# Running the first kernel block's preparation beside the last pass of the stage before it

## The chip, the cores and the metric

The kernel runs on one core of one Trainium2 chip. Times are device microseconds (us) of that core, from the first to the last instruction. "Before" and "changed" are the two kernels. Every number comes from timed runs or from the profile of one execution; a profiled execution lasts about as long as an unprofiled one. TensorE's *granted clock* is given as a share of full speed.

## The reference, cut to what matters

```python
def forward(x, w_r, w_i, A_re, A_im, B_re, B_im, C_re, C_im, log_dt, Dskip, gate_w):
    g = sigmoid((x * gate_w).sum(-1, keepdims=True))
    # 2D stage: a spectral filter over sequence (2048) and channels (1024)
    a = irfft2(rfft2(x) * (w_r + 1j * w_i))
    # kernel loop: K[d,l] = Re sum_n C dB exp(dt A l), then a long convolution
    K = einsum("dn,dnl,dn->dl", Cc, exp(dt * A * l), dt * Bc).real
    b = irfft(rfft(x, 4096) * rfft(K, 4096))[:2048] + x * Dskip
    return g * a + (1 - g) * b
# the kernel returns this function's gradients for grad_out
```

The kernel first does the 2D stage, forward and backward. Then a loop over eight blocks of 128 channels builds `K`. The change is at the seam of the two.

## The kernel before

The 2D stage ends with its backward half. `middle(True)` multiplies the spectra and writes one gradient, `gw`, to memory. `last_bwd` is the last pass, 16 steps. In each step TensorE runs 8 matmuls for step h+1 and 4 for step h; VectorE and ScalarE evict one half each of the first product, and ScalarE evicts the second product.

```python
def last_d(bwd, h):
    ...  # 8 matmuls of V and DP into pd
    Ue = wps["Ue"].tile([P, 2, 512], dt.bfloat16, name="Ue", bufs=2)
    nc.vector.tensor_copy(out=Ue[:, 0, :], in_=pd[:, 0, :])
    nc.scalar.activation(out=Ue[:, 1, :], in_=pd[:, 1, :], func=ACT.Copy)
    return Ue

def last_n(bwd, h, Ue):
    ...  # 4 matmuls of B1, nB1 and Ue into pa
    och = wps["och"].tile([P, D], dt.bfloat16, name="och", bufs=2)
    nc.scalar.activation(out=och[:], in_=pa[:].rearrange("p a b -> p (a b)"), func=ACT.Copy, ...)
    nc.sync.dma_start(out=scr.rearrange("(r h) d -> r h d", h=H16)[:, h, :], in_=och[:])

def last_bwd():
    Ue = last_d(True, 0)
    for h in range(H16):
        nxt = last_d(True, h + 1) if h + 1 < H16 else None
        last_n(True, h, Ue)
        Ue = nxt
...
    open_pools(s2_, ("a_mid2", ("Xf", "gw", "Z", ...)), ("a_last", ("Ue", "och")))
    middle(True)
    last_bwd()
```

The memory of all that is handed to the kernel loop when the stage ends. Only then does the loop prepare block 0: `OP` (decays times sines, 9 operations on VectorE and 6 sines on ScalarE), `EA` (32 exponentials on ScalarE), the weights `wb` (on GpSimd, from a table that a transfer brings into `bc`), `wO` (`OP` times `wb`, 5 operations on VectorE), and `AN` in four units.

```python
def weights(bi, OP):
    bc = kw.tile([P, 4, P], dt.bfloat16, name="bc", bufs=1)
    nc.gpsimd.dma_start(out=bc[:], in_=nlb_scr[2:6, :, dsl]...)
    dtk = kw.tile([P, P], dt.float32, name="dtk", bufs=1)
    nc.gpsimd.dma_start(out=dtk[:], in_=dt_scr[:, dsl])
    TTp(out=bc[:, 0:2, :], in0=bc[:, 0:2, :], in1=dtk..., op=ALU.mult)
    ...  # seven more small operations on GpSimd give wb and wv
    wO = kw.tile([P, 2, NA, P], dt.bfloat16, name="wO")
    nc.vector.tensor_tensor(out=wO[:], in0=OP[:], in1=wb[:, 0:2, :]..., op=ALU.mult)
    ...  # two more products and sums on VectorE
    return wO
...
AN = new_an()
OP = sin_o(0, EO)
EA = exps_a(0)
wO = weights(0, OP)
for q in range(4):
    sin_a(0, q, AN, EA)
for bi in range(DC):        # block bi runs on TensorE while block bi+1 is prepared
    ...
```

## Time and profile before

| | before |
|---|---|
| median of 3 runs | 1442.45 us (1437.49 to 1445.57) |
| profiled span | 1437.5 us |
| backward middle stage, first product to its last copy | 295.9 to 396.7 |
| last backward pass, to the start of its last eviction | 396.7 to 441.9 |
| block 0's first transpose on TensorE | 478.4 |
| block 0 done on TensorE: its first `KT` on VectorE | 516.5 |

No engine bounds the whole. The first part of the page of the kernel before gives busy time, share of the span and number of instructions by engine:

```profile
PE 1070.7 (74%) x7161; PEld 736.9 (51%) x7187; DVE 1143.5 (80%) x1897; ACT 841.8 (59%) x1279; POOL 239.2 (17%) x489
```

So one reads the seam by stretches. This is the busy time by stretch, kernel before; the first row names the columns.

```profile
core 0: us, PE busy (x) PEld busy (x) DVE busy (x) ACT busy (x) POOL busy (x), PEclk, DMA share, GB/s
287.00:400.00 113.00, 93.97 (x573) 52.72 (x580) 78.28 (x180) 43.77 (x49) 23.38 (x50) 1.00 0.63 115
400.00:443.00 43.00, 40.08 (x183) 23.37 (x184) 12.93 (x21) 24.39 (x33) 21.11 (x36) 1.00 0.39 132
443.00:478.00 35.00, 0.00 (x0) 0.00 (x0) 29.36 (x25) 29.63 (x50) 11.32 (x11) 0.50 0.55 216
478.00:520.00 42.00, 21.33 (x142) 17.22 (x142) 36.27 (x37) 32.84 (x58) 9.71 (x11) 0.54 0.37 129
```

In the pass (second stretch) TensorE is busy 40 of 43 us and VectorE only 13. In the third stretch TensorE does nothing at all, while VectorE and ScalarE prepare block 0. In the fourth, block 0 runs at about half the clock.

The timeline of the kernel before shows single instructions: start, duration, engine and line, output and input, and in brackets the idle time before it and what ended that.

```profile
394.33 0.82 POOL L857 DMA_DIRECT2D bc<-nlb_scr  x1
...
404.79 0.69 DVE L495 CAST Ue<-p 128x512 bf16<-128x512 f32 x1 [1.97 <-PE p L492]
...
405.52 0.60 ACT L496 ACTIVATE Ue<-p 128x512 bf16<-128x512 f32 x1 [1.15 <-DVE Ue L495]
406.01 1.02 ACT L506 ACTIVATE och<-p2i 128x1024 bf16<-128x1024 f32 x1
406.55 0.56 POOL L870 TENSOR_SCALAR wv<-wv 128x128 f32<-128x128 f32 x1
...
442.90 1.28 ACT L123 ACT_TABLE_LOAD   x1
444.20 1.04 ACT L123 ACTIVATE OP<-ti__4270,pi_b 128x896 bf16<-128x896 uint16 x1
...
478.41 0.33 PE L888 MATMUL trp<-ident,AN 128*128 128x128 bf16 x1 [36.64 <-DVE AN L818]
```

The last row is the prize: TensorE waits 36.6 us for `AN`. The first row: GpSimd asks for block 0's table at 394, so `wb` is ready at about 406, long before anybody wants it.

In the middle stage VectorE waits for the following; the view of the waits of the kernel before, 295.87 to 396.69, gives for each line and releaser the us in total, the number and the longest:

```profile
DVE UV L638 <- ACT UV L640: 18.9, 6, 3.2
DVE m L594 <- ACT Gs L586: 8.5, 6, 5.2
DVE gw L607 <- DMA out_dram<-gw: 1.8, 1, 1.8
DVE m L594 <- DMA out_dram<-gw: 0.6, 2, 0.3
```

### The profile page before, as it was taken

What the parts mean: (1) busy time and instruction counts of PE and PEld (TensorE: products, weight loads), DVE (VectorE), ACT (ScalarE), POOL (GpSimd) and SP (SyncE); (2) the same over time, 40 slices, a digit from 0 to 9 for tenths busy, and PEclk for the clock granted to TensorE, in tenths of its full rate; (3) what the DMA queues carried; (4) which work ended last, traced back from release to release, by engine and by line L of the source; (5) the groups of instructions that cost most, each with busy time, mean ns of one, the idle gap of its engine ahead of it and who ended that gap; (6) DMA issues with size and microseconds to landing.
All of it is one profiled execution on the core that took longest, in us unless ns stands there. A gap on an engine that the chain in (4) does not pass through costs nothing. (4 is left out here: it accounts for less than half of the span.)

```text
span 1437.5 us, 20147 instructions
## 1 busy us (share of the span) xinstructions
PE 1070.7 (74%) x7161; PEld 736.9 (51%) x7187; DVE 1143.5 (80%) x1897; ACT 841.8 (59%) x1279; POOL 239.2 (17%) x489
## 2 busy tenths in 40 slices
PE   3968887688892356856964979688898887688973
PEld 1434444344451244645752756466666654566752
DVE  5668999667726979788878887388999999789997
ACT  2563455534358687686687554356666564677750
POOL 5101110012251312101100010301203032122110
PEclk9879999899996556855965958899999998699996
DMA  4445574247646242434432547888979664887751
GB/s 146 154 131 158 167 214 169 110 119 122 104 121 255 81 150 88 156 147 147 180 132 95 193 157 242 286 124 161 215 132 282 72 209 73 257 318 262 244 165 30
DMA packets 153067, 236.06 MB, mean 164 GB/s; under 512 B 26371, under 2 KB 100739, under 8 KB 149766
## 3 DMA queue, kind: packets, MB, share of 16 engines
q1 hardware_dynamic: 133766, 184.95, 45.4%
q0 software_dynamic: 12960, 48.25, 10.9%
q10 hardware_dynamic: 6240, 1.57, 0.5%
q8 instruction: 56, 0.92, 0.3%
q14 instruction: 45, 0.37, 0.2%
HBM read 126.80 MB, written 107.66 MB: 163 GB/s over the span
## 5 line engine op out<-in xcount | busy, mean ns | idle before, releaser
L889 PE MATMUL pK<-wO,AN 128*128 128x84 bf16 x512 | 101.0, 343 | 23.2 <-DVE st L997 21.0
L1066 ACT ACTIVATE Vt<-f 128x1024 bf16<-128x1024 f32 (+1 forms) x72 | 64.5, 930 | 91.5 <-PE f L1155 52.9
L888 PE MATMUL trp<-ident,AN 128*128 128x128 bf16 x512 | 76.3, 277 | 47.3 <-DVE AN L818 41.5
L1434 DVE TENSOR_TENSOR pd<-Tsb,ORJ 128x5376 bf16<-128x5376 bf16 x32 | 94.0, 2949 | 8.2 <-PE pr L1440 7.0
L924 PE MATMUL kx<-Kc,TK 128*128 128x256 bf16 x680 | 96.0, 284 | 2.7 <-DVE spk L932 1.5
L1321 ACT ACTIVATE Tsb<-pT 128x704 bf16<-128x704 f32 x112 | 76.7, 754 | 26.2 <-PE pT L1315 26.0
L889 PEld LDWEIGHTS <-AN 128*128 128x128 bf16 x512 | 75.7, 151 | 29.5 <-issue 24.2
L888 PEld LDWEIGHTS <-AN 128*128 128x128 bf16 x512 | 61.3, 159 | 55.7 <-DVE AN L818 42.9
L1164 PE MATMUL pq<-TKT,PY 128*128 128x321 bf16 x544 | 85.7, 304 | 0.8 <-DVE PY L1134 0.6
L549 PE MATMUL p<-TD,UV 128*128 128x512 bf16 x240 | 66.0, 400 | 24.0 <-DVE Y L553 16.0
L1440 PE MATMUL pr<-pd,ident 128*128 128x256 bf16 x504 | 70.6, 292 | 16.4 <-DVE pd L1434 16.3
L1066 ACT ACTIVATE XG<-f 128x1024 bf16<-128x1024 f32 (+1 forms) x72 | 68.2, 983 | 23.0 <-PE f L1104 9.3
L1191 PE MATMUL f<-Vr,S1i 128*128 128x256 bf16 x256 | 69.1, 389 | 6.6 <-DVE Vr L1072 6.6
L924 PEld LDWEIGHTS <-TK 128*128 128x128 bf16 x680 | 62.8, 101 | 20.9 <-issue 4.3
L629 PE MATMUL p2i<-T,Z 128*128 128x512 bf16 x224 | 60.4, 390 | 9.8 <-DVE Z L596 4.4
L1315 PEld LDWEIGHTS <-A2t 128*128 128x128 bf16 x512 | 47.3, 105 | 38.3 <-issue 25.7
L1164 PEld LDWEIGHTS <-PY 128*128 128x128 bf16 x544 | 53.4, 99 | 25.8 <-DVE PY L1134 1.6
L1440 PEld LDWEIGHTS <-ident 128*128 128x128 bf16 x504 | 51.3, 105 | 27.9 <-DVE pd L1434 14.7
L997 DVE CAST st<-pK 128x1024 bf16<-128x1024 f32 x40 | 48.6, 1218 | 19.7 <-PE pK L992 19.5
L1121 DVE TENSOR_TENSOR m<-XG,kb 128x1024 bf16<-128x1024 bf16 (+1 forms) x80 | 46.8, 606 | 20.8 <-ACT XG L1066 16.2
L1315 PE MATMUL pT<-BD,A2t 128*128 128x176 bf16 x448 | 52.0, 251 | 12.8 <-ACT Tsb L1321 7.5
L492 PE MATMUL p<-DP,UV 128*128 128x512 bf16 x250 | 61.1, 385 | 0.6 <-DVE UV L638 0.3
(833 smaller groups left out, 3161.5 us busy)
## 6 DMA issues: line engine op xcount, KB each, us to landing
at<-A SPq DMA_DIRECT2D x32, 512.0 KB, 2.6
st<-st SPq DMA_DIRECT2D x64, 256.0 KB, 2.9
A2t<-at SPq DMA_DIRECT2D x32, 512.0 KB, 7.5
Sg<-st SPq DMA_DIRECT2D x24, 512.0 KB, 7.9
on_scr<-OP SPq DMA_DIRECT2D x8, 1344.0 KB, 8.2
ORJ<-on_scr POOLq DMA_DIRECT2D x8, 1344.0 KB, 9.2
spk<-spk SPq DMA_DIRECT2D x64, 128.0 KB, 1.8
kb<-spk SPq DMA_DIRECT2D x32, 256.0 KB, 5.4
```

Of the source, the lines that this page charges most:

```text
L492: nc.tensor.matmul(pd[:, eo, :], lhsT=V[:, eo * 2 + c_, b_, :, :].rearrange("p k n -> p (k n)")[:, h::H16], rhs=DP[:, eo * 2 + c_, b_, :], ...
L549: nc.tensor.matmul(ps[:, eo, :], lhsT=U[:, dc, (eo * K16 + k1r) * P:(eo * K16 + k1r + 1) * P], rhs=TD[:, dc, eo, :], start=(dc == 0), stop ...
L888: nc.tensor.transpose(trp[:, comp, cc, :], AN[:, comp, :, c], ident[:, :])
L889: nc.tensor.matmul(pK[:, c4, cc * 4 * NA:(cc + 1) * 4 * NA], lhsT=AN[:, comp, :, c], rhs=wO[:, comp, :, c::32].rearrange("p a q -> p q a") ...
L924: nc.tensor.matmul(px[:, comp, :], lhsT=TK[ci][:, k1, comp, :], rhs=Kc[:, ci, :], start=(ci == 0), stop=(ci == 4 and comp == 1))
L1066: nc.scalar.activation(out=out, in_=in_, func=ACT.Copy)
L1164: nc.tensor.matmul(pq[:, half, 0:NLG // 2], lhsT=PY[:, k_, comp, 256:384], rhs=TKT[:, p0 + k_, comp, half * (NLG // 2):(half + 1) * (NLG / ...
L1191: nc.tensor.matmul(py[:, hh, :, :], lhsT=S1i[:, f_, :], rhs=Vr[:, :, 2 * (hq * HQ + hh) + f_, :], start=False, stop=(f_ == 1), skip_group_ ...
L1315: nc.tensor.matmul(pT[:, cc, 0:4 * NX], lhsT=A2[:, comp, cl * N:(cl + 1) * N], rhs=BD[:, c0_ + cc, :, :].rearrange("p q x -> p (q x)"), st ...
L1321: nc.scalar.activation(out=to_, in_=ti_, func=ACT.Copy)
L1434: TT(out=pd[:], in0=Tsb[:, k_].rearrange("p (g a) d -> p g a d", g=2)[:, :, 0:NA, :], in1=O_.unsqueeze(1).to_broadcast([P, 2, NA, P]), op= ...
L1440: nc.tensor.matmul(pr[:], lhsT=idt[:], rhs=pd[:, :, a_, :], start=(k_ == 0 and a_ == 0), stop=(k_ == 1 and a_ == NA - 1))
```

## The change

The tiles of the last pass move to memory that outlives the 2D stage (a pool `late`, into which the loop's `TK` tables are loaded after the pass). So the loop's memory is free before the pass. `EA` and `OP` of block 0 are written into the program behind the middle stage. `last_bwd` becomes a generator, and `wO` and `AN` are woven between its steps. Cut to its core:

```diff
+        late = lctx.enter_context(tc.tile_pool(name="late", bufs=1, ...))
-            DP = ac.tile([P, 4, 2, 512], dt.bfloat16, name="DP")
+            DP = late.tile([P, 4, 2, 512], dt.bfloat16, name="DP")
+            XS = late.tile([P, 4, 2048], dt.int32, name="UV2")      # tables' integers; later UV2, later TK
+            UO = late.tile([P, 4, D], dt.bfloat16, name="UO")
...
-                Ue = wps["Ue"].tile([P, 2, 512], dt.bfloat16, name="Ue", bufs=2)
+                Ue = UO[:, h % 2, :].rearrange("p (a b) -> p a b", a=2)
...
-                och = wps["och"].tile([P, D], dt.bfloat16, name="och", bufs=2)
+                och = UO[:, 2 + h % 2, :]
...
                     last_n(True, h, Ue)
                     Ue = nxt
+                    yield h
...
-                tp = s1_.enter_context(tc.tile_pool(name="a_tmp", bufs=1, ...))
+                # the first tables take their integers from XS; kci, kcf, n2k too
...
+            bctx.close()
+            kps[0] = ectx.enter_context(tc.tile_pool(name="k_prep", bufs=1, side="right", ...))
             with ExitStack() as s2_:
                 middle(True)
-                last_bwd()
+                EA = new_ea()
+                exps_a(0, EA)
+                OP = sin_o(0, EO0)
...
-            OP = sin_o(0, EO)
-            EA = exps_a(0)
+            lb = last_bwd()
+            next(lb)
+            next(lb)
             wO = weights(0, OP)
             for q in range(4):
+                next(lb)
+                next(lb)
                 sin_a(0, q, AN, EA)
+            for _ in lb:
+                pass
+            psctx.close()
+            load_tk()
```

Besides, the skip row is loaded by blocks. Hardly any work is added or removed.

## The prediction

> **What bounds the kernel now.** No engine bounds the whole span: the page's first part has VectorE at 80%, TensorE at 74%, ScalarE at 59%. The change concerns the seam at 400 to 480 us (timeline and busy-time-by-stretch views):
>
> - 400 to 443, the last backward pass: 16 steps of 2.59 us, set by TensorE (busy 40.1 of 43). VectorE is busy 12.9 (a 0.69 us eviction a step, "idle 1.90 <-PE"), ScalarE 24.4.
> - 443 to 478, preparation of kernel block 0: TensorE does nothing. Its first transpose waits 36.6 us for the last product into AN, one of the two longest waits of 400 to 480. VectorE is busy 29.4 of 35, ScalarE 29.6, mostly in series: OP's sines, 32 exponentials (9.9 us), AN's sines.
>
> Afterwards a block takes 42 us, with VectorE busy 36 to 37: close to its limit.
>
> **What the change does.** Almost no work is removed or added; it is moved. The pass's tiles get memory that outlives the 2D stage, so the loop's memory is free before the pass.
>
> - On ScalarE EA's exponentials (9.9 us), OP's six sines (6.2) and two table loads (1.28 each), and on VectorE OP's nine operations (3 x (1.09 + 0.62 + 1.08) = 8.4) can run from about 290 us, when the turn's buffers are free. They fall into the backward middle stage (287 to 400), where ScalarE is idle 69 us and VectorE 35, with a 3.15 us VectorE gap in nearly every 13 us round.
> - wO (2.95 + 4 x 1.55 = 9.2 us) and AN's four units (about 3.1 us VectorE and 2.3 ScalarE each) go beside the pass. They need 22 us of VectorE, which has 30 idle there, and 9 of ScalarE, which has 19. GpSimd has wb by 406 already today.
> - Added: eight small loads of the skip row. The TK loads stay behind the pass; the first spectrum reads TK at 562, so they are free.
>
> **What lies on the critical path.** The TensorE gap from 441.4 to 478.4, 37 us, less:
> - 5 to 6 us by which fillers stretch the pass. Towards VectorE, TensorE has some 1.7 us of slack per step (12 matmuls 2.59, minus 0.69 and signalling): 1.2 us pieces cost little, wO's 2.95 us piece about 1. ScalarE has 1.62 of 2.59 us taken per step; a 1.15 us sine makes it 2.77, some tenths of a us for each of 8 to 14 sines.
> - 1 to 2 us in the middle stage, about 1 us to hand PSUM over.
>
> The first transpose should come at about 448. Some of block 1's OP may also be done beside the pass, worth 2 to 3 us. I expect 31 us in all, and nothing gives it back: the later stages are as busy as before.
>
> Predicted: 1411 us, range 1398 to 1425. Faster by over 2% (below 1413.6): 0.57; within 2%: 0.41; slower by over 2%: 0.02. It stands close to the threshold.
>
> **What would show each step right or wrong.** In the timeline: Exp and OP's sines on ScalarE before 400, the middle stage's rounds still 13.0 us; the pass's steps at 2.6 to 3 us with AN's and wO's work on VectorE between evictions; first AN transpose at 445 to 452, its wait under 5 us; blocks still about 42 us; from the first spectrum on, everything earlier by the same 30 us.
>
> **What would make it wrong.** The new tiles may reuse memory that is released late, so that sines wait after all. Fillers may be put before critical evictions, so that middle or pass grows by 10 us. Blocks 0 and 1 may wait for something else (block 1's sines, a DMA), so that the earlier start ends in a longer block. The reverse: block 1 fully prepared beside the pass, worth up to 8 us more.

## The result, and the profile after

The changed kernel took 1425.67 us (median of 4 runs, 1420.54 to 1426.91); the kernel before 1441.98 in the same rounds (1437.49 to 1445.57). The ratio is 0.9882, with a 95% interval of 0.9845 to 0.9919. A ratio is the mean time of one kernel's fast runs over that of the other's of the same rounds, so it is not quite the ratio of the medians quoted. The gain is 16 us, about half of the 31 predicted: faster, but within 2%. All outputs are right.

The profile answers to the marks shown above. I read them from the timeline, in two traces of the unedited changed kernel (the second comes from the experiment `changed_again`):

| us | before | changed | changed, again | gain (mean) | predicted |
|---|---|---|---|---|---|
| start of the backward middle | 295.9 | 304.2 | 302.9 | -7.7 | 0 |
| backward middle | 100.8 | 108.4 | 106.5 | -6.6 | -1 to -2 |
| last pass, to the start of its last eviction | 45.2 | 60.4 | 60.0 | -15.0 | -5 to -6 |
| pass to block 0's first transpose | 36.6 | -0.3 | -0.3 | +36.9 | +37, less 1 for PSUM |
| block 0, first transpose to `KT` | 38.1 | 28.5 | 28.7 | +9.5 | +2 to +3 |
| sum: first `KT` at | 516.5 | 501.2 | 497.7 | +17.0 | 31 |

The gap on TensorE is gone entirely, and block 0 got faster than I thought. From the end of the middle stage to the first `KT` the kernel gained 31.3 us (119.8 before, 88.6 and 88.3 changed): the predicted number, by another sum. But 7 us were lost within the middle, and 8 before it.

The 8 us can be placed. The 2D stage has a middle in its forward half too, from its first product `m` to its last copy on ScalarE. Its first product comes no later in the changed kernel (105.00 and 104.32 us in the two traces) than before (105.99), and from its end to the start of the backward middle the time is the same (93.3 before, 93.7 and 93.3 changed). The forward middle itself took 96.6 us before and 105.6 and 105.2 changed. Its busy time by stretch, before and changed, with the columns of above:

```profile
105.99:202.57 96.58, 81.18 (x495) 46.24 (x501) 85.61 (x141) 41.21 (x45) 13.26 (x41) 0.96 0.59 166
```

```profile
105.00:210.56 105.56, 87.00 (x529) 48.55 (x528) 94.16 (x151) 43.62 (x48) 12.48 (x43) 0.97 0.58 164
```

VectorE, the third engine, is the busiest in both, and has 8.6 us more to do there in the changed kernel: six more operations on the tables' angles (`ti`), two more `to` and two more copies of `Y`, which lay outside this stretch in the kernel before, fall into it. That fits the 9 us that the stage grew by; no experiment moved this work out again, so the place of the early loss is shown and its cause is only argued.

The busy time by stretch, changed kernel, in the stretches shown of before:

```profile
287.00:400.00 113.00, 88.87 (x496) 48.61 (x495) 83.87 (x181) 57.51 (x85) 18.19 (x41) 0.95 0.58 129
400.00:443.00 43.00, 33.45 (x187) 18.31 (x186) 29.49 (x43) 19.55 (x24) 22.19 (x28) 0.92 0.40 89
443.00:478.00 35.00, 30.03 (x149) 18.56 (x148) 33.82 (x33) 28.67 (x36) 23.57 (x27) 0.95 0.54 197
478.00:520.00 42.00, 30.12 (x210) 25.22 (x209) 28.53 (x33) 34.55 (x65) 7.36 (x8) 0.63 0.62 222
```

TensorE now works in the third stretch. But in the first two its clock fell to 0.95 and 0.92: it stood still somewhere there, and the next view shows where. In the third stretch VectorE is busy 33.8 of 35 us, so it may now bound the end of the pass; the run wb_ready below tests that.

The timeline of the changed kernel around the pass, with start, duration and waits as before:

```profile
414.96 0.82 POOL L871 DMA_DIRECT2D bc<-nlb_scr  x1 [4.96 <-PE p2i L663]
...
421.69 0.68 POOL L874 TENSOR_TENSOR bc<-bc,dtk 128x256 bf16<-128x256 bf16 x1 [5.36 <-DMA dtk<-dt_scr]
...
425.58 0.41 POOL L882 CAST wb<-wv 128x256 bf16<-128x256 f32 x1
...
426.02 2.96 DVE L887 TENSOR_TENSOR wO<-OP,wb 128x5376 bf16<-128x5376 bf16 x1 [5.50 <-POOL wb L882]
...
426.78 2.59 POOL L884 TENSOR_SCALAR wv<-wv 128x128 f32<-128x128 f32 x1
...
429.64 0.61 PE L534 MATMUL p2i<-UO,B 128*128 128x512 bf16 x1 [5.42 <-DVE UO L528]
...
431.32 3.57 PE L525 MATMUL p<-DP,UV 128*128 128x512 bf16 x8
...
438.18 1.89 PE L525 MATMUL p<-DP,UV 128*128 128x512 bf16 x8
...
472.69 0.31 PE L902 MATMUL trp<-ident,AN 128*128 128x128 bf16 x1
```

Read it from the top. The table for `bc` is asked for at 414.96, not at 394, because GpSimd waits there for a matmul of the middle stage (`PE p2i`). So `wb` is ready at 426.0. VectorE stands 5.5 us before `wO`, and the pass's next eviction stands behind `wO` in VectorE's queue: it starts when `wO` ends, at 428.9. TensorE waits 5.4 us for such an eviction, and then runs 8 matmuls in 3.57 us that take 1.89 a little later: its clock was lowered. The last row has no wait in brackets: block 0 starts at once.

"TensorE: Matmul & The Clock Gate" of the Trainium skill (Part 1, *What's actually happening* and *HAM oscillation*) says that an idle window of about 3.4 us halves the clock and about 3.4 us of work restores it, and that a wait for a transfer that crosses the window makes the next tile run cold. This trace agrees: 5.42 us idle, then 3.57 instead of 1.89 us; the first 8 matmuls at full speed again start at 434.73, 5.1 us after work began again (429.64).

And in the middle stage (view of VectorE's waits, changed kernel, 304.23 to 412.62):

```profile
DVE UV L672 <- ACT UV L674: 14.3, 4, 4.2
DVE gw L641 <- DMA out_dram<-gw: 5.9, 3, 3.3
...
DVE m L628 <- DMA out_dram<-gw: 1.6, 1, 1.6
```

The waits for `gw`'s stores have grown from 1.8 and 0.6 to 5.9 and 1.6 us.

### The profile page after: what moved, and what is told of

Read it like the earlier page. It is cut to its first block, busy times and chain, and to the rows that moved or that the text cites. A ratio compares the mean times of both kernels' runs of the same rounds, so it can differ in the third digit from the quotient of the medians.

```text
span 1424.5 us, 20171 instructions
## 1 busy us (share of the span) xinstructions
PE 1083.0 (76%) x7187; PEld 738.5 (52%) x7187; DVE 1143.1 (80%) x1897; ACT 837.9 (59%) x1277; POOL 243.1 (17%) x489
## 5 line engine op out<-in xcount | busy, mean ns | idle before, releaser
L583 PE MATMUL p<-TD,UV 128*128 128x512 bf16 x256 | 69.8, 400 | 18.2 <-DVE Y L587 10.5
L940 PE MATMUL kx<-UV 128*128 128x256 bf16 x408 | 73.4, 292 | 2.0 <-DVE spk L948 1.3
L525 PE MATMUL p<-DP,UV 128*128 128x512 bf16 x256 | 64.4, 392 | 9.7 <-ACT UO L529 9.2
L1008 PE MATMUL pK<-xg,S1f 128*128 128x512 bf16 x80 | 35.3, 538 | 44.2 <-ACT Kq L913 35.5
L663 PE MATMUL p2i<-T,Z 128*128 128x512 bf16 x224 | 60.0, 389 | 10.3 <-ACT UV L674 5.3
L1148 DVE TENSOR_TENSOR m<-XG,kb 128x1024 bf16<-128x1024 bf16 (+1 forms) x80 | 46.8, 606 | 16.5 <-ACT XG L1093 11.8
```

Source lines behind the costliest of these rows:

```text
L525: nc.tensor.matmul(pd[:, eo, :], lhsT=V[:, eo * 2 + c_, b_, :, :].rearrange("p k n -> p (k n)")[:, h::H16], rhs=DP[:, eo * 2 + c_, b_, :], ...
L583: nc.tensor.matmul(ps[:, eo, :], lhsT=U[:, dc, (eo * K16 + k1r) * P:(eo * K16 + k1r + 1) * P], rhs=TD[:, dc, eo, :], start=(dc == 0), stop ...
L940: nc.tensor.matmul(px[:, comp, :], lhsT=TK[ci][:, k1, comp, :], rhs=Kc[:, ci, :], start=(ci == 0), stop=(ci == 4 and comp == 1))
```

## The experiments

My theory after the result was this: (a) the pass is long because of the late `wb`; (b) the middle is long because of the moved work, above all `OP`'s store, which stands in the same queue as `gw`'s; (c) the early loss is a matter of the order of instructions. The rivals: (a') the pass is bound by VectorE, whatever `wb` does; (b') the middle loses to `gw`'s own transfers; (c') the single tile `XS` that all early integers share makes the early part slow. The forward middle was not among the suspects. Twelve kernels ran, 5 rounds each. The results in one table; "before" is the median of the kernel before on the same chip in the same rounds. Two of those medians, 1441.79 and 1451.10, include one run of eleven that was slow (1452.07 and 1459.37); the medians of the fast runs are 1441.09 and 1450.90:

| run | median us | before | ratio (95%) | start of middle | middle | pass | middle's end to first `KT` |
|---|---|---|---|---|---|---|---|
| wb_early | 1424.66 | 1441.79 | 0.9902 (0.9853 to 0.9951) | 302.3 | 107.0 | 58.1 | 85.7 |
| store_late | 1424.51 | 1441.79 | 0.9918 (0.9867 to 0.9970) | 300.7 | 102.5 | 64.3 | 92.6 |
| old_order_one_table | 1441.13 | 1441.79 | 1.0023 (0.9976 to 1.0071) | 296.2 | 101.5 | 45.4 | 120.1 |
| early_repaired | 1423.86 | 1441.79 | 0.9901 (0.9846 to 0.9956) | 298.2 | 107.6 | 59.8 | 88.0 |
| changed_again | 1428.18 | 1439.04 | 0.9914 (0.9878 to 0.9950) | 302.9 | 106.5 | 60.0 | 88.3 |
| scalar_evicts | 1426.15 | 1439.04 | 0.9905 (0.9879 to 0.9932) | 307.1 | 104.7 | 57.3 | 85.1 |
| pass_alone | 1448.22 | 1439.04 | 1.0056 (1.0025 to 1.0086) | 300.4 | 104.2 | 52.4 | 108.0 |
| four_mends | 1413.88 | 1439.04 | 0.9836 (0.9813 to 0.9860) | 293.3 | 109.7 | 53.2 | 80.6 |
| wb_ready | 1430.50 | 1451.10 | 0.9869 (0.9821 to 0.9916) | 299.7 | 114.7 | 57.8 | 81.9 |
| middle_clear | 1441.37 | 1451.10 | 0.9939 (0.9891 to 0.9987) | 303.4 | 105.0 | 68.7 | 97.6 |
| five_mends | 1422.03 | 1451.10 | 0.9810 (0.9757 to 0.9863) | 302.6 | 110.2 | 53.0 | 80.5 |
| four_mends_gw4 | 1404.12 | 1432.74 | 0.9798 (0.9753 to 0.9844) | 303.6 | 100.3 | 54.0 | 81.2 |

Most intervals overlap each other. So the totals of the single repairs tell nothing, and I judge those by the stages in the traces.

### wb_early: GpSimd asks for the table before the pass

When the kernel is built, the program places `bc` at byte 111,392 of each partition, over `T6` (100,512 to 125,088), which the middle stage reads to its end: hence GpSimd's wait for a matmul. Before, it lay over a tile that was long free. Here the GpSimd part of `weights` is split off and placed ahead of the pass's first step, which also moves its memory.

```diff
-            def weights(bi, OP):
+            def weights_b(bi):
                 ...
+                return wb
+            def weights(bi, OP, wb=None):
...
             lb = last_bwd()
+            wb0 = weights_b(0)
             next(lb)
             next(lb)
-            wO = weights(0, OP)
+            wO = weights(0, OP, wb0)
```

> The changed kernel with one difference of memory only: the six small tiles that block 0's B*dt weights are made of (bc, dtk, wb, wv, wa, wc) are asked for before the big AN tile, so that they lie over TD, which the middle stage has last read at about 398 us, and not over T6, which it reads until 414.7. The instruction order on every engine is the same as in the changed kernel. Theory A (the load of bc waited for its memory, and the weights came late by that): bc is issued by about 400 instead of 414.96 us, wb is ready at about 409 instead of 425.99, the 5.50 us wait of VectorE for GpSimd's wb and the 5.42 us wait of TensorE behind it go, and with them the slow clock after it; the last pass ends about 7 us earlier after the middle stage's end (51 instead of 58.3 us) and the program is 5 to 8 us faster than the changed kernel, ratio to the kernel before about 0.983 to 0.985. Rival B (the pass is long because VectorE and ScalarE have too much other work in it, the wait only swallows slack): the wait goes, but the pass still takes over 55 us and the time gains less than 3 us. Rival C: the earlier bc load and the GpSimd work collide with the end of the middle stage and lengthen it by about as much as is won.

The timeline of wb_early:

```profile
406.21 0.18 POOL L632 COPY Z<-Z 128x2 bf16<-128x2 bf16 x1 [3.58 <-DVE Z L631]
406.45 0.82 POOL L871 DMA_DIRECT2D bc<-nlb_scr  x1
...
415.08 0.68 POOL L874 TENSOR_TENSOR bc<-bc,dtk 128x256 bf16<-128x256 bf16 x1 [7.25 <-DMA dtk<-dt_scr]
...
424.33 0.39 PE L534 MATMUL p2i<-UO,B 128*128 128x512 bf16 x1 [3.48 <-DVE UO L528]
```

The memory is no longer waited for, but the request stands in GpSimd's queue behind the last small copy `Z` of the middle stage, at 406.2, which itself waited 3.58 us (the middle of this trace ended at 409.3). From the request to the first use of the table 8.6 us pass. TensorE's wait shrank from 5.4 to 3.5 us (its first matmuls after it still ran at full speed, slow ones began 1.1 us later, at 425.45), and middle's end to `KT` from 88.5 to 85.7. The repair is worth 2 to 3 us. The wait is not gone, so this run could not decide between (a) and (a').

Against "DMA: Bandwidth & Descriptors" of the skill (*Anatomy of one DMA*, about 2.0 us plus bytes over 436,000 per us), 131 KB should land in some 2.3 us, an estimate from that page. It need not fit here: the runs that `bc` is read in are only 256 bytes long. From the request to the first use the traces show 7.1 us (before), 6.7 (changed) and 8.6 (wb_early), with a second, smaller transfer (`dtk`) behind it in the same queue, which the first use waits for as well.

### store_late: the store of OP after gw's stores

```diff
-        nc.sync.dma_start(out=on_scr[bi]..., in_=OP[:]...)
+        st_ = nc.sync.dma_start(out=on_scr[bi]..., in_=OP[:]...)
+        if bi == 0:
+            dep(st_, gw_out[0])      # order only: behind the last store of gw
```

> The changed kernel with one transfer moved: block 0's 1.34 MB store of OP, issued in the middle of the backward middle stage at about 340 us, is held behind the stage's last gw store on the SyncE queue. No other instruction moves. Theory A (that store delays the gw stores, whose buffers VectorE then waits for): the waits of VectorE for the transfer of gw (3.31, 2.45 and 0.17 us in the changed kernel) go back to about the 1.8 us of the kernel before, no gw store takes over 10 us, and the backward middle stage, from its first m to its last ScalarE copy, takes 106 to 107.5 us instead of 110.5; the program is 3 to 4 us faster than the changed kernel. Rival (the exponentials and sines in the stage's ScalarE queue lengthen it): the stage still takes 109 us or more, and only the single gw stores are quicker. The part before 290 us is an exact repeat of the changed kernel and shows the noise of the marks.

The middle took 102.5 us, against 108.4 and 106.5, and VectorE waited 2.8 us for `gw`'s buffers, against 5.9. It looked as if theory (b) was right. But the pass grew to 64.3 us, and four_mends below, with the same edit, had a middle of 109.7 us. Six traces with the changed kernel's store (all but that of wb_ready, whose middle is changed otherwise) lie between 104.2 and 108.4. With the edit the middle took 102.5, 109.7, 110.2 (five_mends) and 100.3 us (four_mends_gw4). So the good middle of this trace can't be put down to the store. One trace of one run would have misled me here.

### old_order_one_table: the old order, with the early integers in one tile

This is the kernel before with a single edit: the early tables take their integers from one tile of four rows, as in the changed kernel.

```diff
                 tp = s1_.enter_context(tc.tile_pool(name="a_tmp", bufs=1, ...))
+                XS = tp.tile([P, 4, 2048], dt.int32, name="XS")   # kci, kcf, n2k in its rows 2 and 3
+                nti = [0]
                 def ints(F):
-                    return tp.tile([P, 2048], dt.int32, name="ti", bufs=2)[:, 0:F]
+                    nti[0] ^= 1
+                    return XS[:, nti[0], 0:F]
```

> The kernel before with one part of the change alone: the integer tables of the early part (ti twice, kc_i, kc_f, n2k1) are slices of one 128x4x2048 tile as in the change; the old seam, pools and order of the last pass are kept. Everything behind the forward middle stage is the same work. Theory A (the one tile gives the scheduler another order in the first 90 us, and that costs the early 4.8 us): the last sine of the tables (bv) comes at 96 to 97 us as in the changed kernel (96.73), not at 91.93, the copy of the wall transposes comes at about 30 instead of 28.23, and the program is 3 to 8 us slower than the kernel before, ratio 1.002 to 1.006. Rival (the order of loads on the SyncE queue, which follows from where the pools lie, does it): bv at 92 to 93 us and the time the same as before within 2 us.

The time is that of the kernel before (1.0023, 0.9976 to 1.0071), and the middle starts at 296.2. So (c') falls: in the old order the shared tile costs nothing that can be measured. It also shows that the marks repeat: 101.5, 45.4 and 120.1 us stand against 100.8, 45.2 and 119.8.

### early_repaired: GpSimd's and the load queue's early order put back

In the changed kernel some early instructions stand in another order than before: GpSimd's small table `cks` comes before the `wall` fills, and loads of `grad_out` come before the first loads of `Wt`.

```diff
-            nc.gpsimd.tensor_scalar(out=cks[:, g:g + 1], ...)
+            ck_ = nc.gpsimd.tensor_scalar(out=cks[:, g:g + 1], ...)
+            for w_ in walls:
+                dep(ck_, w_)
...
-                    nc.sync.dma_start(out=xt[:, hq * 2:hq * 2 + 2, :], in_=(gov if bwd else xv)[:, hs, :])
+                    ld_ = nc.sync.dma_start(out=xt[:, hq * 2:hq * 2 + 2, :], in_=(gov if bwd else xv)[:, hs, :])
+                    if bwd and hg == 0:
+                        dep(ld_, wts_[1])    # behind the second load of Wt
```

> The changed kernel with two orders of the early part put back, without a synchronisation: on GpSimd the first wave of cks and ci_ comes after all the wall memsets, and on the SyncE queue the first loads of grad_out come behind the first four loads of Wt. Theory A (these two orders cost the early 7.7 us): the copy of the wall transposes is back at about 28.2 us (changed kernel 30.23), bv at 92 to 94 us instead of 96.73, the end of the forward middle stage at 203 to 206 instead of 210.56, and the program is 4 to 8 us faster than the changed kernel. Rival (the early part is bound elsewhere, by the stores and loads of the direction tables or the other work mixed into it): the copy comes earlier but bv stays at 95 us or later and the program gains less than 2 us.

Both early marks moved as expected: the copy of the first table is at 26.1 us, against 30.2 in the changed kernel and 28.2 before, and the last early sine (`bv`) at 88.4, against 96.7 and 91.9. But the forward middle then took 108.0 us, and so the gain was lost there. The backward middle starts at 298.2 here, and in the three later kernels with this edit at 293.3, 302.6 and 303.6: a mean of 299.4. Eight traces with the changed early part lie between 299.7 and 307.1, with a mean of 302.6. The two with the old early order have 295.9 and 296.2. A gain of 3 us is smaller than the spread, so it is not shown. That the changed kernel starts its middle some 6.5 us later (302.6 against 296.05) is well supported by these ten traces. In all twelve traces with the changed early part the forward middle took 105.2 to 110.3 us, in the two without it 96.6 and 97.5: the loss lies there, whatever the order before it. Its cause stays open.

### changed_again: the changed kernel, unedited

No edit; it gives a second trace and a second chip.

> The changed kernel itself, unedited, on the same chip as the next three: the yardstick for them, and the noise of the marks. Expected, from its first trace and from the two experiments that repeat its early part: first m of the backward middle stage at 300 to 305 us, that stage to the 1x2048 ScalarE copy 106 to 109 us, the last pass from that copy to its last eviction 58 to 61 us, the first block's transpose of KT 86 to 90 us after that copy, ratio to the kernel before 0.985 to 0.992.

The ratio was 0.9914 (0.9878 to 0.9950), in agreement with the first. Middle and pass were 106.5 and 60.0 us. So pass and middle's end to `KT` (60.4 and 60.0; 88.6 and 88.3) repeat to half a us, while the middle and its start move by 1 to 2 us, and in edited kernels by more.

### scalar_evicts: the pass evicts on ScalarE alone

If VectorE bounds the pass (a'), taking its 16 evictions away should help.

```diff
-                nc.vector.tensor_copy(out=Ue[:, 0, :], in_=pd[:, 0, :])
-                nc.scalar.activation(out=Ue[:, 1, :], in_=pd[:, 1, :], func=ACT.Copy)
+                if bwd:
+                    nc.scalar.activation(out=Ue, in_=pd[:], func=ACT.Copy)
+                else:
+                    ...   # as before
```

> The changed kernel with one difference: in the last backward pass the eviction of p into UO, that VectorE (0.68 us) and ScalarE (0.60 us) did one after the other, is one 128x1024 copy on ScalarE alone (about 1.02 us). VectorE has no part in the pass any more, so its preparation work (wO, AN, OP, 1.2 to 3 us each, in order) can stand before no eviction. Theory A (the pass is stretched because that work and the wait for wb stand in VectorE's queue ahead of evictions): the two long TensorE waits of the pass behind VectorE go (5.4 us in the changed kernel), the steps without a sine take about 2.6 us, those with one about 3.0, the pass takes 47 to 51 us instead of 60, and the first KT comes 6 to 10 us earlier after the middle stage's end than in the changed kernel. Rival B (the pass is bound by the sum of ScalarE's work, or by a slower TensorE clock): it still takes over 55 us. Rival C (the work is only pushed back): the pass is short but the first block's KT comes no earlier.

The pass went from 60 to 57.3 us, middle's end to `KT` from 88.5 to 85.1. The timeline of scalar_evicts shows why it was not more:

```profile
424.96 2.96 DVE L890 TENSOR_TENSOR wO<-OP,wb 128x5376 bf16<-128x5376 bf16 x1 [6.47 <-POOL wb L885]
...
434.78 1.15 ACT L123 ACTIVATE AN<-ti__4110,pi_b 128x1024 bf16<-128x1024 uint16 x1 [7.21 <-DVE ti__4110 L408]
```

The wait for `wb` only changed its path. VectorE waits 6.5 us for `wb`; `AN`'s angles stand behind `wO` on VectorE; the sine of those angles waits 7.2 us on ScalarE; and the evictions of the pass stand behind the sine. Here VectorE's and ScalarE's queues serve both the preparation and the pass, and the wait of the one, 6.5 us on VectorE, came out as 7.2 us on ScalarE for the other.

### pass_alone: the pass with nothing beside it

The pass runs to its end before `wO` and `AN` begin. `OP` and `EA` stay early.

```diff
...   # last_n and last_d keep their last evictions in ev_; weights takes one
             lb = last_bwd()
-            next(lb)
-            next(lb)
-            wO = weights(0, OP)
-            for q in range(4):
-                next(lb)
-                next(lb)
-                sin_a(0, q, AN, EA)
             for _ in lb:
                 pass
+            dep(ev_[1], tail_[0])        # order only: behind the last eviction on ScalarE
+            tail_[0] = ev_[1]
+            wO = weights(0, OP, ev_[0])  # its first product behind the last eviction on VectorE
+            for q in range(4):
+                sin_a(0, q, AN, EA)
```

> The changed kernel with nothing beside the last pass: the sines of AN and of block 1's OP are chained behind the pass's last ScalarE eviction, wO behind its last VectorE eviction. The exponentials and block 0's OP stay in the middle stage. It measures what the overlap inside the pass is worth. Theory A (the preparation beside the pass costs the pass about what it saves later): the pass takes 45 to 46 us as in the kernel before (45.2), the first transpose of AN comes 5 to 9 us after it, and the first KT 84 to 90 us after the middle stage's end, no later than in the changed kernel (88.6); the time is within 3 us of the changed kernel's. Rival B (the overlap is worth the 9.5 us by which block 0 is shorter): the first KT comes 95 us or more after the middle stage's end and the program is 6 us or more slower than the changed kernel.

My expectation was wrong. I thought the overlap in the pass had been worth almost nothing. From the middle's end to `KT` this kernel needs 108.0 us against 88.3, and it is 20 us slower than the changed kernel in the same rounds. The overlap in the pass is worth 19.7 us, the early `OP` and `EA` 11.8 (119.8 less 108.0). TensorE again waits for `AN` (timeline of pass_alone):

```profile
474.15 0.32 PE L905 MATMUL trp<-ident,AN 128*128 128x128 bf16 x1 [17.26 <-DVE AN L416]
```

The pass took 52.4 us here, 60.0 in the changed kernel; so the woven work lengthens it by some 7.6 us. Of the 52.4, 5.1 are still a wait of TensorE behind `wb`: I had held back only the first product of `wO`, and a second one, `wt_`, slipped in between two evictions and waited 7.4 us there. So the experiment is not quite pure, and the remaining growth over 45.2 is mostly that wait.

### wb_ready: the table asked for in the middle stage

To settle (a) against (a'), the whole of `weights_b` is done in the middle stage, in memory of its own. Now `wb` is there when the pass begins.

```diff
                 middle(True)
                 EA = new_ea()
                 exps_a(0, EA)
                 OP = sin_o(0, EO0)
+                w0p = s2_.enter_context(tc.tile_pool(name="k_w0", bufs=1, side="right", ...))
+                wb0 = weights_b(0, w0p, kps[0].tile([P, 3, P], dt.bfloat16, name="wb0"))
...
-            wO = weights(0, OP)
+            wO = weights(0, OP, wb0)
```

> The changed kernel with the B*dt weights of block 0 really made early: their loads and GpSimd work stand at the start of the backward middle stage, with small tiles of their own in memory that is free there, not after the stage's last Z copy. Run wb_early showed that memory alone moved the load by only 8 us, because GpSimd issues it in order behind that copy and it then takes 7 us to land. Theory A (the wait for wb costs the pass about 5.4 us of idle TensorE, about 1.7 us of slow clock after it and the queue behind it): no TensorE wait over 2 us in the pass, the matmuls after the third eviction take 1.9 and not 3.6 us, the pass takes 51 to 54 us instead of 60, the first KT comes 80 to 83 us after the middle stage's end instead of 88; 5 to 8 us faster than the changed kernel, ratio 0.983 to 0.987. Rival (VectorE's and ScalarE's other work in the pass bounds it): the pass stays over 56 us though the wait is gone.

The wait is gone and the clock in the pass is 1.00, but the pass still takes 57.8 us. The busy time by stretch of each kernel's pass tells the reason; the kernels are, one fence each, before, changed, pass_alone, scalar_evicts and wb_ready.

```profile
396.70:441.90 45.20, 43.24 (x196) 24.94 (x198) 12.93 (x21) 25.75 (x35) 21.11 (x36) 1.00 0.42 124
```

```profile
412.60:473.00 60.40, 48.38 (x202) 25.56 (x202) 49.38 (x48) 41.90 (x51) 42.66 (x49) 0.94 0.45 142
```

```profile
404.60:457.00 52.40, 45.15 (x196) 25.21 (x198) 15.93 (x19) 25.98 (x35) 23.10 (x38) 0.93 0.43 123
```

```profile
411.80:469.10 57.30, 47.57 (x207) 26.51 (x210) 39.16 (x30) 47.25 (x51) 40.75 (x49) 0.94 0.44 134
```

```profile
414.40:472.20 57.80, 49.07 (x228) 28.53 (x231) 54.84 (x53) 44.40 (x53) 34.66 (x38) 1.00 0.51 153
```

VectorE's busy time, the third engine in each row, is the one to read. It is 12.9 us before, 49.4 changed, and 54.8 of 57.8 in wb_ready. With the wait gone VectorE is busy 95% of the pass: as soon as `wb` no longer holds it up, it fills the time with block 1's `OP`, `wO` and part of its `AN`. Rival (a') is right about what bounds the pass then: five_mends below, with wb_ready's edit and the evictions on ScalarE besides, has a pass of 53.0 us. Theory (a) is right that the changed kernel waits.

That work is not lost: middle's end to `KT` fell to 81.9 us, 6.6 less than in the changed kernel. But the middle took 114.7 us. The only edit in it is GpSimd's work for `wb`; by what path it costs 7 us there is open.

### middle_clear: no foreign work in the middle stage

```diff
-                nc.scalar.activation(out=V[0:1, 0, 1, :, :], in_=ps[:], func=ACT.Copy)
+                mid_end[0] = nc.scalar.activation(out=V[0:1, 0, 1, :, :], in_=ps[:], func=ACT.Copy)
...
                 EA = new_ea()
+                dep(mid_end[0], tail_[0])    # order only: EA and OP behind the middle stage
+                tail_[0] = mid_end[0]
                 exps_a(0, EA)
```

> The changed kernel with the exponentials of EA and the sines of block 0's OP chained behind the last ScalarE instruction of the backward middle stage, so that nothing foreign but one early integer product stands in that stage. Theory A (the foreign work delays the stage's rounds and lets TensorE idle long enough to fall to the slow clock): the stage takes 100.5 to 103 us as in the kernel before, with no dip of the granted clock inside it; the other seven traces of the changed form have 102.5 to 109.7. Rival (the stage is longer for the pools' new places or the queue order, not for the foreign work): it still takes 105 us or more. In both cases the pass begins about 10 us late behind the 32 exponentials, and the program is 0 to 8 us slower than the changed kernel.

With `EA`'s exponentials and `OP`'s sines all behind it, the middle still took 105.0 us, with 6.0 us of waits for `gw`'s stores at the same operation as in the changed kernel. So theory (b) falls as the main cause: without the moved work most of the growth is still there, 4.2 us over the 100.8 of the kernel before, against 7.6 and 5.7 in the changed kernel. This is one trace, and the other changed kernels with two buffers for `gw` range from 102.5 to 114.7; a share of 1.5 to 3.4 us (106.5 and 108.4 less 105.0) for that work can't be excluded. The pass, with that work in it, grew to 68.7 us: doing it in the middle is right.

### four_mends, five_mends: the repairs together

four_mends has the edits of wb_early, store_late, early_repaired and scalar_evicts; five_mends has wb_ready's in place of wb_early's.

> The changed kernel with four mends at once: the early orders put back, block 0's store of OP behind the gw stores, the small tiles of the weights over TD, and the evictions of the last pass on ScalarE alone. If the losses are those that the single experiments show and they add up: first m of the backward middle stage at about 297 us, the stage 102 to 103 us, the pass 47 to 50, the first KT at 475 to 482 us instead of 501, and the program 18 to 24 us faster than the changed kernel, ratio to the kernel before 0.971 to 0.977, that is about what was predicted for the change. If they do not add up, because what comes earlier meets the same later wait (wb, or the loads of TK), the first KT comes after 487 us and the ratio is above 0.98.

> The kernel of four_mends with the weights of block 0 made in the middle stage as in wb_ready in place of their move over TD. Of the pass of four_mends, 53.2 us, 3.0 and 1.2 us were TensorE waits that led back to wb. Expected: pass 48 to 50 us, first KT 75 to 78 us after the middle stage's end instead of 80.6, the program 3 to 5 us faster than four_mends, ratio to the kernel before 0.979 to 0.983. If ScalarE, now with two evictions of 1.02 us and a sine of 1.1 in a step, is the bound, the pass stays at 52 us or more and nothing is won.

four_mends took 1413.88 us, 0.9836 (0.9813 to 0.9860), against 0.9914 (0.9878 to 0.9950) for the unedited changed kernel on the same chip: these intervals do not overlap. Middle's end to `KT` is 80.6 us. In its pass ScalarE is the busiest engine, no longer VectorE (busy time by stretch, four_mends, with the columns of before; the first two rows are places in its middle stage, the last is the pass):

```profile
333.30:343.30 10.00, 5.75 (x21) 2.09 (x21) 5.95 (x15) 2.05 (x2) 0.76 (x6) 0.78 0.80 121
373.30:383.30 10.00, 6.95 (x32) 3.62 (x32) 5.17 (x12) 2.21 (x4) 0.56 (x3) 0.83 0.26 67
403.00:456.20 53.20, 45.93 (x206) 26.14 (x209) 39.32 (x30) 47.07 (x50) 42.16 (x47) 1.00 0.57 169
```

ScalarE is busy 47.1 of 53.2 us in the pass, and the clock stays at 1.00. five_mends does no better from the middle's end on (80.5), as `wb` no longer matters there, and its middle is long too (110.2). Its ratio, 0.9810 (0.9757 to 0.9863), is not to be told from four_mends'.

In the two places of the middle stage TensorE is busy 5.8 and 7.0 of 10 us, at a clock of 0.78 and 0.83. Transfers hold VectorE up there (view of the waits, four_mends, 293.3 to 403.03):

```profile
DVE gw L653 <- DMA out_dram<-gw: 5.1, 3, 3.3
DVE m L652 <- DMA Xf<-xs_scr: 2.3, 1, 2.3
```

The timeline tells the two places apart. In the second, VectorE waits 3.34 us for `gw`'s store, until 373.31, and TensorE then stands idle for 3.45. In the first, TensorE's idle time of 2.82 us stands behind a wait of 2.25 us for the load of `Xf`, until 339.87; the waits for `gw`'s stores there are 0.68 us before it and 1.12 after it.

### four_mends_gw4: four buffers for gw

The only edit to four_mends; the order of instructions on every engine is the same in both.

```diff
-                        gw = wps["gw"].tile([P, 2, KW], dt.bfloat16, name="gw")
+                        gw = wps["gw"].tile([P, 2, KW], dt.bfloat16, name="gw", bufs=4)
```

> The kernel of four_mends with one difference: gw of the backward middle stage has four buffers instead of two; the instruction order on every engine is the same. Theory A (the stage is longer than in the kernel before because VectorE waits for the stores of gw to give their buffers back, 5.1 us in four_mends, and TensorE, idle meanwhile, then runs at a slow clock): no wait of VectorE for a transfer of gw is left, no slice of the stage has a granted clock under 0.95, the stage takes 101 to 104 us instead of 109.7, and the program is 4 to 7 us faster than four_mends, ratio to the kernel before 0.978 to 0.981. Rival (the waits for gw hide others that come at the same moments: loads of Wt or Xf on the same queue): the wait moves to m <- Wt or Xf and the stage takes 106 us or more.

The middle took 100.3 us, against 109.7 in four_mends and 100.8 before. In the view of VectorE's waits of four_mends_gw4 (303.63 to 403.97) no row for the operation `gw` is left, none for `Xf`, and a short wait of another operation for `gw`'s store:

```profile
DVE m L640 <- DMA out_dram<-gw: 0.8, 1, 0.8
```

The same places of the middle stage (busy time by stretch, four_mends_gw4; its middle starts 10.3 us later, so the stretches do too):

```profile
343.60:353.60 10.00, 7.73 (x41) 3.74 (x40) 7.33 (x19) 3.56 (x4) 0.78 (x6) 1.00 0.73 127
383.60:393.60 10.00, 8.30 (x44) 3.92 (x42) 6.98 (x19) 4.03 (x5) 2.78 (x3) 1.00 0.93 132
```

The clock is 1.00 and TensorE is busy 7.7 and 8.3 us. So (b') is right in this: with two buffers for `gw` the middle stage loses some 9 us that it does not lose with four, partly in waits for `gw`'s stores (5.1 us), partly by the lowered clock. That the wait for `Xf` went too shows that the edit did more than take these waits away; by what path is not shown. This is one trace of each kernel, but it is a single edit, the waits are gone from the view, and among the changed kernels no other middle is shorter than 102.5.

The skill's "Trainium Kernel Development and Optimization" (*Best Practices*) advises to double-buffer so that transfers overlap with compute. Here two buffers were too few: 5.1 us of waits at the operation `gw` with two, and with four 0.8 us at another operation. The kernel before has the same two, and waits only 2.4 us.

This kernel is the best: 1404.12 us (1400.55 to 1412.13) against 1432.74 on its chip, 0.9798 (0.9753 to 0.9844). It beats the kernel before by 28.6 us; as the interval reaches from under to over 0.98, a gain of 2% is not certain. Its ratio is also lower than both of the changed kernel's, whose intervals (from 0.9845 and from 0.9878 upward) it does not touch, the first only just; each is against the kernel before on its own chip. Against four_mends the intervals overlap, and the two profiled spans are alike (1405.5 and 1405.8): the late start of the middle in this trace (303.6 against 293.3) took back what the middle gained. So the gain of this last edit is shown in its stage, not in the total. And the evictions on ScalarE alone and the four buffers could be given to the kernel before as well. That was not tried, so part of the 28.6 us may not belong to the moved work at all.

## Why the prediction was right or wrong

**Right.** The gap of 37 us on TensorE was on the critical path and vanished completely; that the exponentials and sines fit into the idle time of the middle stage held as well (pass_alone puts their worth at 11.8 us, middle_clear shows no lengthening of the middle by them that is clear of the spread). The "about 1 us to hand PSUM over" is not to be seen: the first transpose starts at 472.69, 0.3 us before the last eviction of the pass (472.98).

**Wrong: "5 to 6 us by which fillers stretch the pass".** It was 15.0. Three terms in it failed.
- "They need 22 us of VectorE, which has 30 idle there." I counted `wO` and `AN` of block 0. In the traces block 1's work follows in VectorE's queue, and VectorE does it in the pass too. The pass held 36.5 us (changed, 49.38 less 12.93) to 41.9 us (wb_ready, 54.84 less 12.93) of foreign work, not 22. With the 12.93 of its own that exceeds the 45 us of the pass.
- "GpSimd has wb by 406 already today." True of the kernel before, but the change gave `bc` another place in memory, over a tile that the middle stage reads to the end. `wb` came at 426.0, VectorE stood 5.5 us and TensorE 5.4 us. My list of what would make it wrong had this in general ("memory that is released late"), for sines; I did not apply it to the transfer.
- "TensorE has some 1.7 us of slack per step." The two halves of an eviction run one after the other (0.69 and 0.60 us), so of 2.59 us at most 1.3 are left, an estimate from these three durations.

pass_alone divides the growth: 52.4 less 45.2 is 7.2 us almost without overlap, mostly the wait behind `wb`, and 7.6 us come from the woven work.

**Wrong: "1 to 2 us in the middle stage", rounds "still 13.0 us".** It was nearly 7 us. Mostly it was not the fillers, as I had feared: 4.2 us of it were there without them. Waits for `gw`'s stores grew (1.8 us before, 5.9 changed), and four buffers took the loss away. Why these stores come back later in the changed kernel is open. It can't be put down to the store of `OP`, and to the moved work on ScalarE at most in part.

**Wrong: nothing was expected to move before the seam.** The prediction has no term for the early part at all. There 7.7 us were lost. They were lost inside the forward middle (96.6 us before, 105.6 and 105.2 changed). The one tile for the integers is not the cause (97.5 with it). Nor is it the lateness of the last early sine (`bv` at 91.9 before, 96.7 and 96.1 changed): early_repaired brought `bv` to 88.4, and its forward middle still took 108.0. VectorE has 8.6 us more work in that stage in the changed kernel, and it is the busiest engine there; that this is the cause is likely, and not tested.

**Wrong in my favour: "2 to 3 us" from block 1, "blocks still about 42 us".** Block 0, from its first transpose to `KT`, took 28.5 instead of 38.1 us. It is the same mis-sizing seen from the other side: the work of block 1 that lengthened the pass was missing in block 0. In pass_alone, without it, block 0 takes 38.5 us.

**"Nothing gives it back."** From the first `KT` to the end the kernel before needs 921.0 us and the changed ones 923.3 and 929.8. Other edits, none of which touches that part, range from 920 to 937. No loss can be told from that spread, and none of the experiments was aimed at it.

So the sum of 31 was 37 - 15 + 9.5 - 7 - 8 = 17. With the eviction on ScalarE, the earlier table, four buffers for `gw` and the other two edits of four_mends, the kernel gains 28.6 us. That this is near 31 confirms nothing: it is another kernel and another sum.

## What to carry to other kernels

When work is woven into a stage with idle engines, do not count only the work that you name, but all that stands behind it in the engine's queue: here VectorE did 36.5 to 41.9 us of it in the pass, not the 22 counted, and then set the pace. After moving tiles, look at what each tile's new place overlaps, transfers first: here one request that waited for memory cost VectorE 5.5 and TensorE 5.4 us, and ScalarE some 6. Before you look for the cause of a loss, find the stage in which it lies: two experiments here looked for a loss at the very start that the marks of one more stage place in the forward middle. And judge a repair of a few us by several traces and by the stage it is meant for: one lucky trace supported a wrong cause here.

## What the Trainium skill lacked or had wrong

- "TensorE: Matmul & The Clock Gate", Part 1: an idle window of about 3.4 us halves the clock. In four_mends the clock was also low after shorter breaks: at 341 single matmuls of 512 columns took 0.61 to 0.63 us, against 0.38 at full clock, after idle times of 1.17 and 2.82 us with 1.24 us of work between. So two breaks close together were enough, neither of them 3.4 us long. The page's section on depth-cycling says that frequent short idle times make the clock swing, but not how short or how close together.
- "GPSIMD Engine Reference", 1. Specifications, says that GpSimd shares its memory interfaces with VectorE; that row gives no size. The skill says more of this sharing elsewhere, but has no figure for an operation like this one. Here the same operation on `wv` (128x128) took 0.56 us while VectorE was idle (before, at 406.55) and 2.59 us beside VectorE's `wO` (changed, at 426.78), and ended 0.39 us after `wO` did.
- "DMA: Bandwidth & Descriptors", *Anatomy of one DMA*: about 2.3 us for a transfer of 131 KB from GpSimd is the page's estimate. Here 6.7 to 8.6 us passed from the request to the first use, with other transfers under way and a second one behind it. A figure for a loaded queue, and for a source read in runs of 256 bytes, is missing.
- "ScalarE: Activation LUTs", *What ACT_TABLE_LOAD costs*: 1.28 us for the load and 1.38 us for draining. The load took 1.28 us here, but the sine began 1.30 us after the load's start (442.90 and 444.20), and the load 0.02 us after the eviction before it ended. No draining can be seen.
- "Trainium Kernel Development and Optimization", *Best Practices*: it advises two buffers and has no way to tell when two are too few. `gw` waited 5.1 us with two buffers; with four, 0.8 us of waits for its stores were left, at another operation.
